# The small transfers of a recurrent attention chain, issued by GpSimd instead of ScalarE and SyncE

## The chip, the cores and the metric

The kernel runs on one core of a Trainium2 chip. The metric is the device time of one launch in microseconds. The core has five engines with instruction queues of their own: TensorE (PE; its weight loads are shown as PEld), VectorE (DVE), ScalarE (ACT), GpSimd (POOL) and SyncE (SP, which only issues transfers here). A transfer is issued by one of these queues and carried by 16 shared DMA engines. SPq, ACTq and POOLq in the profile are the issuing instructions of those queues.

## The reference

Two branches read the same normalised input `xn = layernorm(x)`, 2048 rows of 1024, and the result is `x + A(xn) + B(xn)`.

Branch A is attention with a recurrent memory over 64 segments of 32 rows:

```python
for s in range(64):
    h = concat([mem, xs])                     # 8 memory rows + 32 rows of the segment
    q, k, v = h@Wq, h@Wk, h@Wv                # 1024 -> 32 heads x 128
    p = softmax(mask(q@k.T * 128**-0.5))      # 40 x 40 per head
    o = (p@v) @ Wo
    mem = o[:8];  out[s] = o[8:]              # the memory of the next segment
```

Every segment needs the memory that the one before it produced, so the 64 segments are a chain. Each of the four weight matrices has 4096 x 1024 bf16 elements, 8.4 MB.

Branch B picks the 2 rows of `xn` with the highest score `xn@w_r`, passes them through a gated MLP (1024 to 3584 and back) and adds the two results to their rows.

## The kernel before

**Prologue.** Layer norm of 16 tiles of 128 rows, the transposes of `xn` and of `x + xn`, stored to DRAM as `xT_d` (segment inputs) and `zT_d` (the residual, to be added to each segment's output), then branch B, whose two rows are patched into `zT_d`.

**Weights.** The four matrices are cut into 64 granules of 128 x 2048 bf16 (512 KB). 42 stay in SBUF for the whole chain (tiles `wres`, `N_RES = 42`); the other 22 don't fit and are read from DRAM again in every segment, into tile `g`, a pool of six slots (`N_SLOT = 6`). Those 22 are spread evenly over the order of use. `used(g)` issues the next such load right after the matmuls of a streamed granule, so the queue of loads runs at most six ahead of their use. All these loads are issued by SP at line 248.

**One segment** (loop `for s in range(NSEG)`): six phases of eight granules, in the order Q first half, K first half, Q second half, K second half, V first half, V second half (`PHASES`); each granule is four matmuls (L510) that fill a `PSm` bank. Then the output projection with Wo, 16 granules (L549). Smaller steps hang between the granules as hooks, `hook(phase, kc, fn)`: they run after granule `kc` of that phase. The scores of the first 16 heads come at (2, 5), those of the second half at (4, 5); the weighted sums with V at (5, 2), (5, 5) and inside the Wo loop. At the end `OB` is copied from PSUM (L575, L576), its memory rows are transposed and put into the next segment's input `ST` (L267).

**Left rows.** A tile has 32 columns: 24 rows of the segment and 8 of the memory. The remaining 8 rows of four segments are put together as 32 "left" rows (`STL`) and projected for a whole group of four segments at a time. The position in a group is `j = s % 4`. In the segment with j = 1 the left rows of the next group go through Wq, with j = 2 through Wk (extra matmuls at L514), with j = 0 those of the own group go through Wv. The projected left rows are transposed (`transposes_left`, L421), copied to `QS` (L424, ACT), stored to DRAM in `qkl_d` (L426) and read back segment by segment as `QKL` (L357). `QKL` is read by a POOL copy into the right-hand columns of `KT` (L432), and the score matmuls (L436, L438) need that copy.

**The small transfers of the chain**, per segment: four stores of `OB` to the output (L579, 12 KB each), one load of the residual `ZT` (L394, 64 KB), one of the next input `ST` (L260, 64 KB), two of `QKL` (L357, 64 KB each). In two segments of four, two stores of `QS` (L426, 128 KB each); once per group a load of `STL` (L351, 64 KB) and four stores of `OL`, the left rows' output (L596, 16 KB each). Stores of outputs are issued by SP, between the weight loads; the others by ACT, between its PSUM copies.

**Order and waits.** The order on each engine is the order of the program text (`manual_schedule`), and every queue is strictly in order: an instruction that waits holds everything behind it. The completion of transfers is counted on semaphores. There are eight of them for the transfers that SP and ACT issue together (DMAHW0 to DMAHW7 in the order rows), and eight more for those of POOL (DMASW0 to DMASW7). They are handed out in turn, and a transfer waits before its issue until the one that had the same semaphore before it has landed.

Of the kernel before, what the change touches and what calls it, by code (L numbers as in the profile page):

```python
# [25 lines left out]
def kernel(  # L26
# [16 lines left out]
    nc = tc.nc  # L43
# [4 lines left out]
    SEG = int(A_seg_len)  # L48
# [8 lines left out]
    XM = SEG - M  # L57
# [4 lines left out]
    out2 = out[0]  # L62
# [32 lines left out]
    xT_d = [dram.tile([4, P, KC * SEG], BF16, name=f"xT_d{t}") for t in range(NT)]  # L95
    zT_d = dram.tile([NSEG + 1, P, KC, SEG], BF16, name="zT_d")
    stl_d = [dram.tile([P, KC * SEG], BF16, name=f"stl_d{t}") for t in range(NT)]
    qkl_d = [dram.tile([2, 2, P, 4, P], BF16, name=f"qkl_d{t}") for t in range(NT)]
# [158 lines left out]
        fetch()  # L257
    def load_st(s):
        ST = stp.tile([P, KC, SEG], BF16, tag="st", name="ST")
        nc.scalar.dma_start(out=ST.rearrange("p k r -> p (k r)"), in_=xT_d[s // 4][s % 4])  # L260
# [87 lines left out]

    def load_stl(g):
        STL = one.tile([P, KC, SEG], BF16, tag="stl", name="STL")  # L350
        nc.scalar.dma_start(out=STL.rearrange("p k r -> p (k r)"), in_=stl_d[g][:, :])  # L351
        return STL

    def load_qkl(s, half):

        t = two.tile([P, 2, P], BF16, tag="qkl", name="QKL")
        nc.scalar.dma_start(out=t[:, :, :], in_=qkl_d[s // 4][:, half, :, s % 4, :].rearrange("m p c -> p m c"))  # L357
# [12 lines left out]

    for s in range(NSEG):
# [19 lines left out]

        def fetch_z():
            Zt = nxt["z"] = one.tile([P, KC, SEG], BF16, tag="zt", name="ZT")
            nc.scalar.dma_start(out=Zt[:, :, :], in_=zT_d[s])  # L394

        def split_z():
            Zt = nxt["z"]
# [3 lines left out]
        def fetch_st():  # L401
            if s + 1 < NSEG:
                nxt["st"] = load_st(s + 1)
# [14 lines left out]
        def transposes_left(mat, half, XB, g):  # L418
            PTq = psT.tile([P, 4, 4, 32], BF16, tag="t", name="PTq")
            for il in range(4):  # L420
                nc.tensor.transpose(out=PTq[:, il, :, :].rearrange("p j r -> p (j r)"), in_=XB[:, il * P:(il + 1) * P],  # L421
                                    identity=IDENT[:, :])
            QS = two.tile([P, 4, 16, XL], BF16, tag="xb", name="QS")
            nc.scalar.copy(out=QS.rearrange("p s h r -> p h s r"),  # L424
                           in_=PTq.rearrange("p i j (s r) -> p (i j) s r", s=4))
            nc.scalar.dma_start(out=qkl_d[g][mat, half].rearrange("p s c -> p (s c)"),  # L426
                                in_=QS.rearrange("p s h r -> p (s h r)"))

        def scores(half):
            QKL = load_qkl(0, half) if s == 0 else QKLs.pop(0)  # L430
            q, k = QT[half], KT[half]
            nc.gpsimd.tensor_copy(out=k[:, :, 32:NK], in_=QKL[:, 1, :].rearrange("p (h r) -> p h r", r=XL))  # L432
# [70 lines left out]
        for p, (mat, half) in enumerate(PHASES):  # L503
            PSm = psA.tile([P, 512], F32, tag="acc", name="PSm")
            PSl = psL.tile([P, 512], F32, tag="accl", name="PSl") if mat in left else None
            for kc in range(KC):
                g = 8 * p + kc
# [12 lines left out]
            if mat < 2:  # L520
                XB = two.tile([P, 512], BF16, tag="xb", name="XB")
                nc.scalar.copy(out=XB[:, :], in_=PSm[:, :])  # L522
                hooks.setdefault((p + 1, 1), []).insert(0, lambda m=mat, h=half, b=XB: transposes(m, h, b))
                if PSl is not None:
                    XBl = two.tile([P, 512], BF16, tag="xb", name="XBl")
                    nc.vector.tensor_copy(out=XBl[:, :], in_=PSl[:, :])
                    hooks.setdefault((p + 1, 3), []).insert(
                        0, lambda m=mat, h=half, b=XBl, g=left[mat]: transposes_left(m, h, b, g))
            else:
                c0 = half * 512  # L530
                VM[half] = one.tile([P, 512], BF16, tag="vm", name="VM")
# [44 lines left out]
        nc.vector.tensor_copy(out=OB[:, P:256], in_=WO[:, P:256])  # L576
        def store(OB=OB, s=s):
            for g in range(4):
                nc.sync.dma_start(out=out2[s * SEG:s * SEG + XM, 256 * g:256 * (g + 1)],  # L579
                                  in_=OB[32 * g:32 * g + XM, :])  # L580

        todo = [store]
# [6 lines left out]
        if j == 3:  # L589
            OL = one.tile([P, 256], BF16, tag="pm", name="OL")  # L590
            nc.scalar.copy(out=OL[:, :], in_=WL[:, 0:256])

            def store_left(OL=OL, G=G):
                o4 = out2[4 * G * SEG:4 * (G + 1) * SEG, :].rearrange("(s r) d -> s r d", s=4)
                for g in range(4):
                    nc.sync.dma_start(out=o4[:, XM:SEG, 256 * g:256 * (g + 1)], in_=OL[32 * g:32 * (g + 1), :])  # L596
            todo.append(store_left)
        if s + 1 < NSEG:
            ST = nxt["st"]
# [37 lines left out]
```

## Time and profile before

| | |
|---|---|
| median of 3 runs | 2555.86 us (2551.04 to 2556.03) |
| the profiled execution | 2564.14 us, span 2562.2 us |
| PE busy | 1865.3 us, 73% of the span |
| ACT / DVE / POOL busy | 513.5 / 638.4 / 108.0 us |
| moved by DMA | 831.71 MB, mean 325 GB/s |
| of these, SP's queue (q1) and ACT's (q10) | 800.19 MB and 26.25 MB |
| first and last `OB` copy | 234.5 and 2553.9 us |

The profile's page has the totals, the queues, a chain of waits that leads to the end, and groups of instructions. Beside it the trace can be asked for waits by who waited for whom, for a timeline of one engine, and for the busy time and the transfer rate in chosen windows. In the windows the "DMA share" is the mean busy share of the 16 DMA engines; it can read a few hundredths over 1 because packets overlap. A busy PE is partly a matter of modelled ends, and a wait for several semaphores is put down to the one that came last.

### The profile page before, as it was taken

How to read it: one execution, taken by the hardware profiler on the slowest of the kernel's cores; microseconds unless marked ns; L12 is line 12 of the kernel's file. 1: busy time of each engine (PE TensorE's matmuls, PEld its weight loads, DVE VectorE, ACT ScalarE, POOL GpSimd, SP SyncE). 2: the span in 40 equal slices, each digit the busy share in tenths (PEclk: the TensorE clock that was granted, in tenths of full speed). 3: DMA queues.
4: the chain of work that ended last, by engine and by line, in shares of the span. 5: the costliest groups of instructions: out<-in, count | busy, mean ns of one | idle time of the engine just before them, and what ended most of it. 6: DMA issues, size and time to landing. Idle time of an engine off the chain costs nothing.

```text
span 2562.2 us, 82489 instructions
## 1 busy us (share of the span) xinstructions
PE 1865.3 (73%) x36873; PEld 975.1 (38%) x36873; DVE 638.4 (25%) x1733; ACT 513.5 (20%) x1145; POOL 108.0 (4%) x371
## 2 busy tenths in 40 slices
PE   4366777777777777677777777777776877777676
PEld 3233343344334334333433343343333433343333
DVE  5302222222222222222222222222232222222222
ACT  4202122121212212111221212122121221122111
POOL 4200000000000000000000000000000000000000
PEclk9568989898989989988898988999899988889889
DMA  9997999999999989989998999999998998999898
GB/s 333 298 353 244 341 320 323 316 351 340 311 332 326 340 297 328 335 299 334 329 349 302 344 322 321 341 330 339 313 334 309 360 320 302 334 327 340 320 336 293
DMA packets 368855, 831.71 MB, mean 325 GB/s; under 512 B 69458, under 2 KB 122738, under 8 KB 368500
## 3 DMA queue, kind: packets, MB, share of 16 engines
q1 hardware_dynamic: 303668, 800.19, 87.3%
q10 hardware_dynamic: 64832, 26.25, 3.8%
q8 instruction: 288, 4.72, 0.7%
q14 instruction: 67, 0.55, 0.1%
HBM read 804.28 MB, written 22.02 MB: 322 GB/s over the span
## 4 chain that ended last, share of the span: by engine, by line
DMA 62%; PE 27%; issue 4%; DVE 3%; ACT 2%; SPq 2%; ACTq 1%; POOL 0%; DVEq 0%; POOLq 0%
DMA g<-in_A_Wv_dram 15%; DMA g<-in_A_Wq_dram 14%; DMA g<-in_A_Wo_dram 13%; PE PSm L510 12%; DMA g<-in_A_Wk_dram 6%; PE WO L549 4%; PE PSl L514 3%; DMA qkl_d<-QS 2%; DMA QKL<-qkl_d 2%; PE WL L549 2%; DMA ZT<-zT_d 2%; PE PTq L408 1%; DMA ST<-xT_d 1%; SPq L248 1%; DMA zT_d<-Tz 1%
## 5 line engine op out<-in xcount | busy, mean ns | idle before, releaser
L510 PE MATMUL PSm<-wres,ST 128*32 128x512 bf16 x8192 | 785.2, 423 | 15.7 <-DVE ST L267 13.6
L510 PE MATMUL PSm<-g,ST 128*32 128x512 bf16 x4096 | 450.9, 427 | 325.8 <-DMA g<-in_A_Wk_dram 136.0
L510 PEld LDWEIGHTS <-ST 128*32 128x32 bf16 x12288 | 329.0, 101 | 770.2 <-issue 413.8
L549 PEld LDWEIGHTS <-OT 128*32 128x32 bf16 x8192 | 224.8, 102 | 170.5 <-issue 150.9
L522 ACT CAST XB<-PSm 128x512 bf16<-128x512 f32 x256 | 150.2, 587 | 660.6 <-PE PSm L510 535.2
L549 PE MATMUL WO<-wres,OT 128*32 128x256 bf16 x5120 | 248.2, 293 | 17.3 <-issue 17.3
L549 PE MATMUL WO<-g,OT 128*32 128x256 bf16 x3072 | 169.1, 294 | 99.6 <-DMA g<-in_A_Wo_dram 83.8
L514 PE MATMUL PSl<-wres,STL 128*32 128x512 bf16 x2048 | 210.4, 398 | 2.7 <-DMA STL<-stl_d 2.7
L488 ACT CAST OT<-OP 128x256 bf16<-128x256 f32 x256 | 95.5, 373 | 324.6 <-PE OP L485 324.6
L448 ACT ACTIVATE SPS<-SPS 128x320 f32<-128x320 f32 x128 | 54.0, 422 | 528.4 <-DVE SPS L447 503.7
L416 DVE COPY KT<-PTq 128x512 bf16<-128x512 bf16 x128 | 54.4, 425 | 348.9 <-PE PTq L408 348.6
L408 PE MATMUL PTq<-IDENT,XB 128*128 128x128 bf16 x1024 | 112.9, 240 | 35.6 <-ACT XB L522 33.6
L446 DVE TENSOR_REDUCE NM<-SPS 128x8 f32<-128x320 f32 x128 | 63.0, 492 | 302.0 <-PE SPS L441 302.0
L432 POOL COPY KT<-QKL 128x128 bf16<-128x128 bf16 x128 | 37.3, 291 | 2335.4 <-PE WO L549 1057.4
L490 DVE CAST OTL<-OP 128x64 bf16<-128x64 f32 x128 | 28.8, 225 | 406.8 <-ACT OT L488 406.8
L408 PEld LDWEIGHTS <-XB 128*128 128x128 bf16 x1024 | 64.2, 104 | 166.2 <-ACT XB L522 131.5
L413 DVE COPY QT<-PTq 128x512 bf16<-128x512 bf16 x128 | 53.2, 416 | 261.1 <-PE PTq L408 261.0
L514 PEld LDWEIGHTS <-STL 128*32 128x32 bf16 x3072 | 86.3, 100 | 70.8 <-issue 14.0
L483 PE MATMUL OP<-PT,VM 32*128 32x40 bf16 x2048 | 94.9, 180 | 19.3 <-ACT VM L532 14.4
L514 PE MATMUL PSl<-g,STL 128*32 128x512 bf16 x1024 | 105.2, 397 | 0.0
L483 PEld LDWEIGHTS <-VM 32*128 32x128 bf16 x2048 | 66.2, 92 | 94.9 <-issue 58.7
L485 PE MATMUL OP<-PT,VL 32*128 32x40 bf16 x2048 | 88.1, 176 | 4.2 <-ACT VL L534 4.2
(99 smaller groups left out, 1513.4 us busy)
## 6 DMA issues: line engine op xcount, KB each, us to landing
g<-in_A_Wq_dram SPq DMA_DIRECT2D x384, 512.0 KB
g<-in_A_Wo_dram SPq DMA_DIRECT2D x384, 512.0 KB
g<-in_A_Wk_dram SPq DMA_DIRECT2D x320, 512.0 KB
g<-in_A_Wv_dram SPq DMA_DIRECT2D x320, 512.0 KB
qkl_d<-QS ACTq DMA_DIRECT2D x64, 128.0 KB
QKL<-qkl_d ACTq DMA_DIRECT2D x128, 64.0 KB
g<-in_B_w_gate_dram SPq DMA_DIRECT2D x16, 448.0 KB
g<-in_B_w_up_dram SPq DMA_DIRECT2D x16, 448.0 KB
```

What stands on the lines that cost most here:

```text
L408: nc.tensor.transpose(out=PTq[:, il, :, :].rearrange("p j r -> p (j r)"), in_=XB[:, il * P:(il + 1) * P], identity=IDENT[:, :])
L413: nc.vector.tensor_copy(out=QT[half][:, :, :], in_=pv)
L416: nc.vector.tensor_copy(out=KT[half][:, :, 0:32], in_=pv)
L446: nc.vector.tensor_reduce(out=NM[:, :], in_=S8, axis=AX.X, op=ALU.max, negate=True)
L448: nc.scalar.activation(out=S8, in_=S8, func=ACTF.Exp, scale=SCALE)
L483: nc.tensor.matmul(o, lhsT=VM[half][q0:q0 + 32, il * P:(il + 1) * P], rhs=PTm[q0:q0 + 32, il, 0:NK], start=True, stop=False, tile_position ...
L485: nc.tensor.matmul(o, lhsT=VL[q0:q0 + 32, c0:c0 + P], rhs=PTl[q0:q0 + 32, il, 0:NK], start=False, stop=True, tile_position=(q0, 0), skip_g ...
L488: nc.scalar.copy(out=OT[half][:, 2 * ph:2 * ph + 2, :, :], in_=ov[:, :, :, 0:SEG])
L510: nc.tensor.matmul(PSm[32 * jq:32 * jq + 32, :], lhsT=ST[:, kc, :], rhs=Gv[:, 512 * jq:512 * (jq + 1)], start=(kc == 0), stop=(kc == KC - ...
L514: nc.tensor.matmul(PSl[32 * jq:32 * jq + 32, :], lhsT=STL[:, kc, :], rhs=Gv[:, 512 * jq:512 * (jq + 1)], start=(kc == 0), stop=(kc == KC - 1),
L522: nc.scalar.copy(out=XB[:, :], in_=PSm[:, :])
L549: nc.tensor.matmul(PS[32 * g:32 * g + 32, 0:256], lhsT=lhs(h), rhs=Gv[:, D * hs + 256 * g:D * hs + 256 * (g + 1)], start=False, stop=(last ...
```

## The change

Seven `dma_start` calls move to the GpSimd queue, with the same operands and at the same places of the program:

```diff
 def load_st(s):
-    nc.scalar.dma_start(out=ST..., in_=xT_d[s // 4][s % 4])
+    nc.gpsimd.dma_start(out=ST..., in_=xT_d[s // 4][s % 4])
 def load_stl(g):
-    nc.scalar.dma_start(out=STL..., in_=stl_d[g][:, :])
+    nc.gpsimd.dma_start(out=STL..., in_=stl_d[g][:, :])
 def load_qkl(s, half):
-    nc.scalar.dma_start(out=t[:, :, :], in_=qkl_d[s // 4][:, half, :, s % 4, :]...)
+    nc.gpsimd.dma_start(out=t[:, :, :], in_=qkl_d[s // 4][:, half, :, s % 4, :]...)
 def fetch_z():
-    nc.scalar.dma_start(out=Zt[:, :, :], in_=zT_d[s])
+    nc.gpsimd.dma_start(out=Zt[:, :, :], in_=zT_d[s])
 def transposes_left(mat, half, XB, g):
-    nc.scalar.dma_start(out=qkl_d[g][mat, half]..., in_=QS...)
+    nc.gpsimd.dma_start(out=qkl_d[g][mat, half]..., in_=QS...)
 def store(OB=OB, s=s):            # four per segment
-    nc.sync.dma_start(out=out2[...], in_=OB[32 * g:32 * g + XM, :])
+    nc.gpsimd.dma_start(out=out2[...], in_=OB[32 * g:32 * g + XM, :])
 def store_left(OL=OL, G=G):       # four per group
-    nc.sync.dma_start(out=o4[...], in_=OL[32 * g:32 * (g + 1), :])
+    nc.gpsimd.dma_start(out=o4[...], in_=OL[32 * g:32 * (g + 1), :])
```

PE's and DVE's instructions stay in the order they had. What follows are the order rows of SP and POOL at two places, with the waits that each instruction carries.

SP around the start of the second segment (s = 1), before. `g` is a streamed granule, `OB` the output of the segment that has just ended; PE in the brackets is the release of the slot.

```order
L248 DMA g<-in_A_Wq_dram 128x2048 [waits DMAHW2_49,PE_49]
L248 DMA g<-in_A_Wq_dram 128x2048 [waits DMAHW3_49,PE_49]
L579 DMA out_dram<-OB 24x256 [waits DVE_49]
L579 DMA out_dram<-OB 24x256 [waits DMAHW4_49]
L579 DMA out_dram<-OB 24x256 [waits DMAHW5_49]
L579 DMA out_dram<-OB 24x256 [waits DMAHW6_49]
L248 DMA g<-in_A_Wq_dram 128x2048 [waits DMAHW7_49,PE_49]
L248 DMA g<-in_A_Wk_dram 128x2048 [waits DMAHW1_49,PE_49]
L248 DMA g<-in_A_Wk_dram 128x2048 [waits DMAHW4_49,PE_49]
L248 DMA g<-in_A_Wk_dram 128x2048 [waits DMAHW5_49,DMAHW0_49,PE_49]
```

The same place of the changed kernel:

```order
L248 DMA g<-in_A_Wq_dram 128x2048 [waits DMAHW6_49,PE_49]
L248 DMA g<-in_A_Wq_dram 128x2048 [waits DMAHW7_49,PE_49]
L248 DMA g<-in_A_Wq_dram 128x2048 [waits DMAHW0_49,PE_49]
L248 DMA g<-in_A_Wk_dram 128x2048 [waits DMAHW1_49,PE_49]
L248 DMA g<-in_A_Wk_dram 128x2048 [waits DMAHW2_49,PE_49]
L248 DMA g<-in_A_Wk_dram 128x2048 [waits DMAHW3_49,PE_49]
```

SP has nothing but weight loads left there, and since only they use the eight DMAHW semaphores now, each one waits for the load eight places before it; before, the numbers skip where an ACT transfer had taken a semaphore in between.

POOL in the third segment of a group (s = 2, j = 2), before. `KT<-QKL` is the copy that the score matmuls need, first half and second half.

```order
L432 COPY KT<-QKL 128x16x8 [waits DVE_49,DMAHW7_49,PE_49,Activation_49]
L456 MEMSET PL 128x8x8 [waits DVE_49]
L432 COPY KT<-QKL 128x16x8 [waits DVE_49,DMAHW7_49,PE_49,Pool_49]
L398 COPY ZL<-ZT 128x8x8 [waits DMAHW1_49]
L399 MEMSET ZT 128x8x8 [waits Pool_49]
```

The same segment in the changed kernel; four stores of `OB` (L579) stand directly ahead of the first row.

```order
L394 DMA ZT<-zT_d 128x256 [waits DMASW3_49,PE_49,Pool_49]
L426 DMA qkl_d_120<-QS 128x512 [waits DMASW4_49,Activation_49]
L260 DMA ST<-xT_d_86 128x256 [waits DMASW5_49]
L432 COPY KT<-QKL 128x16x8 [waits PE_49]
L456 MEMSET PL 128x8x8
L357 DMA QKL<-qkl_d_119 128x2x128 [waits DMASW6_49,PE_49,Pool_49]
L426 DMA qkl_d_120<-QS 128x512 [waits DMASW7_49,Activation_49]
L432 COPY KT<-QKL 128x16x8 [waits DVE_49]
L357 DMA QKL<-qkl_d_119 128x2x128 [waits DMASW0_49,PE_49,Pool_49]
L398 COPY ZL<-ZT 128x8x8 [waits DMASW3_49]
L399 MEMSET ZT 128x8x8 [waits Pool_49]
```

Both `KT` copies now stand behind a store of `QS` that waits for an ACT copy of the same phase. (In the after rows the copy's wait for a transfer is not always listed, because POOL has already waited for it earlier in its own order.)

More of the change, by code (lines that the diff above doesn't have):

```diff
@@ L259, in load_st @@
         ST = stp.tile([P, KC, SEG], BF16, tag="st", name="ST")
-        nc.scalar.dma_start(out=ST.rearrange("p k r -> p (k r)"), in_=xT_d[s // 4][s % 4])
+        nc.gpsimd.dma_start(out=ST.rearrange("p k r -> p (k r)"), in_=xT_d[s // 4][s % 4])
         return ST
@@ L350, in load_stl @@
         STL = one.tile([P, KC, SEG], BF16, tag="stl", name="STL")
-        nc.scalar.dma_start(out=STL.rearrange("p k r -> p (k r)"), in_=stl_d[g][:, :])
+        nc.gpsimd.dma_start(out=STL.rearrange("p k r -> p (k r)"), in_=stl_d[g][:, :])
         return STL
@@ L356, in load_qkl @@
         t = two.tile([P, 2, P], BF16, tag="qkl", name="QKL")
-        nc.scalar.dma_start(out=t[:, :, :], in_=qkl_d[s // 4][:, half, :, s % 4, :].rearrange("m p c -> p m c"))
+        nc.gpsimd.dma_start(out=t[:, :, :], in_=qkl_d[s // 4][:, half, :, s % 4, :].rearrange("m p c -> p m c"))
         return t
@@ L425, in transposes_left @@
                            in_=PTq.rearrange("p i j (s r) -> p (i j) s r", s=4))
-            nc.scalar.dma_start(out=qkl_d[g][mat, half].rearrange("p s c -> p (s c)"),
+            nc.gpsimd.dma_start(out=qkl_d[g][mat, half].rearrange("p s c -> p (s c)"),
                                 in_=QS.rearrange("p s h r -> p (s h r)"))
@@ L578, in store @@
             for g in range(4):
-                nc.sync.dma_start(out=out2[s * SEG:s * SEG + XM, 256 * g:256 * (g + 1)],
+                nc.gpsimd.dma_start(out=out2[s * SEG:s * SEG + XM, 256 * g:256 * (g + 1)],
                                   in_=OB[32 * g:32 * g + XM, :])
@@ L595, in store_left @@
                 for g in range(4):
-                    nc.sync.dma_start(out=o4[:, XM:SEG, 256 * g:256 * (g + 1)], in_=OL[32 * g:32 * (g + 1), :])
+                    nc.gpsimd.dma_start(out=o4[:, XM:SEG, 256 * g:256 * (g + 1)], in_=OL[32 * g:32 * (g + 1), :])
             todo.append(store_left)
```

## The prediction

> **What bounds the kernel now.** I read the page first, then SP's waits, the chain, and windows over a few segments.
>
> ```profile
> span 2562.2 us, 82489 instructions
> L510 PE MATMUL PSm<-g,ST 128*32 128x512 bf16 x4096 | 450.9, 427 | 325.8 <-DMA g<-in_A_Wk_dram 136.0
> L549 PE MATMUL WO<-g,OT 128*32 128x256 bf16 x3072 | 169.1, 294 | 99.6 <-DMA g<-in_A_Wo_dram 83.8
> q1 hardware_dynamic: 303668, 800.19, 87.3%
> q10 hardware_dynamic: 64832, 26.25, 3.8%
> L575 ACT CAST OB<-WO x64: 266/267/268, 234.5 to 2553.9; 128x128 bf16<-128x128 f32 x64
> ```
>
> The last row gives the pace: 63 segments in 2553.9 - 234.5 = 2319.4 us, **36.8 us a segment**. PE idles 325.8 + 99.6 = 425 us ahead of matmuls that use streamed weights, 6.6 us a segment; it is late weights, not arithmetic, that PE waits for. Without that a segment's PE path is 36.8 - 6.6 = 30.2 us. The question is why the weights are late, when their queue runs six granules ahead. The windows are one gap-free stretch, one hole at a segment's start, and four whole segments (j = 0, 1, 2, 3); the last three columns are PE clock, DMA share and GB/s.
>
> ```profile
> 1296.00:1312.00 16.00, 11.98 (x286) 6.90 (x289) 2.94 (x11) 3.71 (x10) 0.38 (x2) 1.00 1.04 397
> 1278.00:1281.00 3.00, 2.61 (x44) 1.01 (x36) 0.34 (x1) 1.17 (x2) 0.00 (x0) 1.00 0.63 194
> 1235.00:1272.00 37.00, 29.05 (x610) 15.30 (x609) 8.44 (x24) 7.44 (x17) 0.77 (x5) 0.86 0.90 315
> 1272.00:1307.00 35.00, 27.19 (x556) 13.75 (x548) 9.74 (x26) 7.53 (x17) 1.00 (x5) 0.95 1.00 357
> 1307.00:1343.00 36.00, 28.18 (x555) 14.15 (x548) 9.74 (x26) 7.53 (x17) 1.00 (x5) 0.91 0.95 334
> 1343.00:1381.00 38.00, 27.36 (x607) 14.76 (x597) 8.96 (x26) 6.62 (x16) 1.39 (x7) 0.91 0.95 342
> ```
>
> The engines can move 397 GB/s, but not through a segment, because there are holes. The hole at 1278 is made as follows (SP's timeline, then the chain at the same place):
>
> ```profile
> 1271.98 2.81 SPq L248 DMA_DIRECT2D g<-in_A_Wq_dram  x2
> 1274.84 3.33 SPq L579 DMA_DIRECT2D out_dram<-OB  x4
> 1279.15 0.37 SPq L248 DMA_DIRECT2D g<-in_A_Wq_dram  x1
> ```
>
> ```profile
> 1271.32 6.53 DMA g<-in_A_Wk_dram
> 1277.86 1.98 DMA out_dram<-OB
> ```
>
> SP issued two loads by 1274.8, then the four output stores. The last store was issued at 1277.86, at the end of the first chain row: a weight load had to land first, since the store waits for a semaphore. The next weight load followed at 1279.15. For over 4 us no weights were ordered. The second chain row leads on to an issue of ACT, which waited for an output store in the same way. The totals of SP's waits (total, times, longest):
>
> ```profile
> SPq L248 <- PE PSm L510: 311.7, 364, 6.2
> SPq L248 <- DMA qkl_d<-QS: 174.6, 48, 8.8
> SPq L248 <- DMA QKL<-qkl_d: 136.7, 60, 5.1
> SPq L248 <- DMA ZT<-zT_d: 57.2, 26, 3.5
> SPq L248 <- DMA out_dram<-OB: 26.0, 26, 2.6
> SPq L579 <- DMA g<-in_A_Wk_dram: 66.3, 61, 3.5
> ```
>
> The first row is the wait that has to be: PE has not released the slot. The next four, 174.6 + 136.7 + 57.2 + 26.0 = 394 us, have nothing to do with the weights. A load stands still until a small transfer of ACT or an output store has landed, because both had the same one of eight semaphores. The last row is the store's own wait, with loads behind it.
>
> **What the change removes.** SP keeps only weight loads; each then waits for its slot and for the load eight places back, which has landed whenever a six-slot ring has room. So the 394 us, and the stores' 66, go from SP's queue. They are not gains one for one, since SP is often ahead; what they buy is a stream without holes. The price of a segment is then the larger of two floors.
>
> *Transfers.* The four windows moved 37 x 315 + 35 x 357 + 36 x 334 + 38 x 342 = 49,170 KB, 12.29 MB a segment. At 397 GB/s, the upper bound, that is 31.0 us; at 357, the best whole segment, 34.4. That segment has all kinds of small transfers in it and one hole, 3 us at a share of 0.63, so 1.1 us lost. Without it 35 x 357 / 33.9 = 369 GB/s. I take 369, since it is the same mix: **33.3 us**.
>
> *PE.* 30.2 us, plus what the change adds (below). So the transfers bound, and the gain is 36.8 - 33.3 = 3.5 us, over 63 segments **-220 us**.
>
> The rule of the Trainium skill that speaks against this is in DMA: Bandwidth & Descriptors, section Issuing engines are not separate DMA queues: transfers run on the same 16 engines whoever issues them, so another issuer saves only the sequencer's time. By that rule the sum would be the rival "nothing to gain" below; SP's rows of waits show that the issuer's place in a queue holds up more than its own time here.
>
> **What it adds.** Ten or so POOL issues a segment, of a kind the trace doesn't have. Bounds from the nearest rows: below, the same transfers on SP; above, POOL's longest instruction.
>
> ```profile
> L579 SPq DMA_DIRECT2D out_dram<-OB x256: 302/352/1460, 237.1 to 2556.8; - x128
> L596 SPq DMA_DIRECT2D out_dram<-OL x64: 615/618/773, 352.2 to 2559.3; - x64
> L168 POOL TENSOR_TENSOR XP<-XP,XN 128x1024 bf16<-128x1024 bf16 x16 | 33.9, 2118 | 42.2 <-ACT XN L163 42.2
> ```
>
> Between 0.35 and 2.1 us; I take **x = 1.0 us**, nearer to the issue rows because it is the same work of writing out addresses. For the software path the Trainium skill, DMA: Bandwidth & Descriptors, section Latency and other measured facts, gives about 1 us to the first byte against 0.6; no run here shows it yet.
>
> POOL's time of ten such issues is hidden: it is busy 1.0 us of a 35 us segment (x5 in the windows). What counts is what stands behind them in its queue, the `KT` copies:
>
> ```profile
> 1307.38 0.29 POOL L432 COPY KT<-QKL 128x128 bf16<-128x128 bf16 x1 [22.98 <-DMA g<-in_A_Wq_dram]
> 1316.44 0.59 ACT L424 COPY QS<-PTq 128x512 bf16<-128x512 bf16 x1 [1.51 <-PE PTq L421]
> 1317.37 0.20 PE L436 MATMUL SPS<-KT,QT 128*32 128x40 bf16 x4
> 1326.60 0.59 ACT L424 COPY QS<-PTq 128x512 bf16<-128x512 bf16 x1 [1.68 <-PE PTq L421]
> 1326.88 0.19 PE L436 MATMUL SPS<-KT,QT 128*32 128x40 bf16 x4
> ```
>
> Before, the first copy ran at 1307.4, right when the segment began, 10 us ahead of the scores (1317.4). In an ordinary segment it now follows four stores, `ZT` and `ST`: 6x + 0.3 = 6.3 us, still in time. In the third segment of a group (this one, j = 2) it follows the store of `QS`, which can't be issued before `QS` is copied (1317.03), and the `ST` load: ready at 1317.03 + 2x + 0.3 = 1319.3, so the scores are **2.0 us late**. The second copy, behind the next `QS` store, is ready at 1327.19 + x + 0.3 = 1328.5, **1.6 us late**. 3.6 us in each of 15 such segments: 54 us of PE time, whose path there becomes 30.2 + 3.6 = 33.8 against the transfers' 33.3. Loads go on while PE stands, until six slots are full, so about half of it shows: **+25 us** (bounds 0 and 54). The reads of `QKL`, `ZT`, `ST` and `STL` are ordered several us or a segment ahead, and a start 1 us later is hidden by the phases between.
>
> The ends are exposed. At s = 0 the first `QKL` is stored and read back while the scores wait, two transfers each about 1.5 us slower: +3. At the end:
>
> ```profile
> 2554.54 2.67 SPq L579 DMA_DIRECT2D out_dram<-OB  x4
> 2557.31 2.63 SPq L596 DMA_DIRECT2D out_dram<-OL  x4
> ```
>
> Eight issues in 5.4 us become eight in 8: +3. ACT loses its issues, which took it little, and its waits for semaphores with them; I credit nothing, as it bounds nothing.
>
> **The sum**, against the profiled execution's own 2564: 2564 - 220 + 25 + 6 = 2375. That execution is 2564.14 - 2555.86 = 8 us above the median of the runs, so **2367 us**, 7% faster.
>
> **The rivals.**
>
> *The stream was at its limit already* (faster, but little). q1 and q10 together fill 91.1% of the engines' time, and two of the four windows read 334 and 342 GB/s at a share of 0.95. If closing the holes only makes more transfers compete, the rate stays near 342 and a segment costs 35.9 us: 0.9 x 63 = 57 us less, 2564 - 57 + 31 - 8 = 2530. For it: the 16 us at 397 had hardly a small transfer in them. Against: the window at 1272 has them all and reaches 357.
>
> *GpSimd becomes the bound* (slower). The place is the first `KT` copy. It is late in ordinary segments from 6x + 0.3 > 10, x = 1.6, and PE's path reaches the old 36.8 us when the delay is 6.6: x = 2.7 is where it decides. At x = 3 it is 18.3 - 10 = 8.3 us late, 30.2 + 8.3 = 38.5 a segment, +1.7 x 63 = 107, with 20 for the ends 2564 + 127 - 8 = 2683. For it: POOL is one queue, and nothing in it may pass an issue. Against: x would lie above the upper row. The mechanism that could bring it there is VectorE, busy 9.74 of 35 us in the window at 1272, if its copies keep POOL from writing descriptors. In the Trainium skill, SBUF — State Buffer, section Who interferes with whom, a VectorE copy in a two-port mode shuts GpSimd out, and a software transfer of about 620 ns is said to have taken 3100 ns beside one. No trace here shows such a pair yet.
>
> *Nothing to gain* (the change does what it says, but SP's waits were harmless). SP saves 256 x 0.352 + 64 x 0.618 = 130 us of its own time, and a segment keeps 36.8 us because PE's releases, the 311.7 row, take the place of the semaphores: 2564 + 31 - 8 = 2587 with what is added, 2556 if that is hidden. Against: the hole at 1278 ends with a load that stood behind stores, and at the releases alone SP waited less than at the semaphores (311.7 against 394).
>
> That it doesn't do what it says is excluded: the order rows show the stores and loads in POOL's queue and none in SP's.
>
> **Chances.** Forecast (2290 to 2450) 0.63; stream at its limit (2450 to 2550) 0.17; GpSimd the bound 0.12; nothing to gain 0.08, split evenly between the same and slower. About 0.2% is what a measurement of this kernel can tell from no change: 2551 to 2561. So faster 0.80, same 0.04, slower 0.16. The range: 31.0 us a segment for the transfers and PE's 30.2 can't both be met without either waiting for the other now and then; half-way between 31.0 and 33.3, 32.2 a segment, gives 2564 - 290 + 31 - 8 = 2297, and I put the low end at 2290. The high end, 2550, takes in the second case.
>
> **What would show it.** In the profile of the changed kernel: a queue of software descriptors with q10's packets and the stores', q10 left with the four loads of the initial memory; POOL's issues with their durations, which decide x; SP's waits with only PE rows at L248 and none for `qkl_d`, `QKL`, `ZT` or `out`; no hole at the segment's start; a pace of 33 to 34 us; PE's idle time ahead of L510 and L549 on `g` cut to less than half of 425 us. Wrong steps would show as follows: the rate, by segments without holes at 340 GB/s and PE still waiting for `g`; x, by POOL issues over 1.6 us and a large row of PE at L436 waiting for POOL's L432; the third segments, by that row with about 15 x 3.6 us if right. The prediction as a whole is wrong if SP's waits for small transfers vanish and the pace doesn't move.

## The result and the profile after

The changed kernel takes 2307.23 us (median of 4 runs, 2291.36 to 2311.28) against 2555.95 us of the kernel before beside it: a ratio of **0.9016 [0.8969, 0.9063]**, 249 us less. The forecast was 2367 us with a range of 2290 to 2550.

From the page after: the span, the queues, the two groups of matmuls on streamed weights and the groups of the new POOL issues.

```profile
span 2309.0 us, 82539 instructions
q1 hardware_dynamic: 292148, 795.98, 93.2%
q0 software_dynamic: 22016, 30.48, 3.9%
q10 hardware_dynamic: 64, 0.02, 0.0%
...
L510 PE MATMUL PSm<-g,ST 128*32 128x512 bf16 x4096 | 421.1, 398 | 111.7 <-DMA g<-in_A_Wq_dram 52.8
L549 PE MATMUL WO<-g,OT 128*32 128x256 bf16 x3072 | 164.6, 285 | 66.4 <-DMA g<-in_A_Wo_dram 53.8
L579 POOL DMA_DIRECT2D out_dram<-OB x256 | 130.4, 516 | 662.9 <-DVE OB L576 662.8
L357 POOL DMA_DIRECT2D QKL<-qkl_d x128 | 91.8, 717 | 520.3 <-issue 377.9
L426 POOL DMA_DIRECT2D qkl_d<-QS x64 | 36.2, 565 | 449.8 <-ACT QS L424 437.4
```

All small transfers went to the software queue; ACT's queue kept the load of the initial memory alone. PE's idle time ahead of streamed weights fell from 425 to 111.7 + 66.4 = 178 us. An issue on POOL takes 0.52 to 0.72 us.

The pace, from the first and last copy of `OB` after:

```profile
L575 ACT CAST OB<-WO x64: 266/266/268, 229.5 to 2297.0; 128x128 bf16<-128x128 f32 x64
```

63 segments in 2067.5 us, **32.8 us each** (before 36.8, 2319.4 us). The profiled executions took 2564.14 and 2310.86 us, 253 us apart, and 252 of them lie between these two copies. Outside them the stretch up to the first copy is 5.0 us shorter and the one behind the last copy 3.7 us longer (12.0 against 8.3 us).

The same long window of the loop, before and after (busy time of PE, PEld, DVE, ACT, POOL, then PE clock, DMA share, GB/s):

```profile
235.00:2220.00 1985.00, 1497.91 (x30124) 769.92 (x30124) 490.50 (x1350) 391.39 (x899) 54.25 (x268) 0.90 0.93 327
```

```profile
235.00:2220.00 1985.00, 1560.45 (x33854) 828.18 (x33847) 545.90 (x1511) 428.97 (x1010) 419.90 (x920) 0.96 1.00 368
```

The rate rose from 327 to 368 GB/s; a segment moves the same, 36.8 x 327 = 12.03 MB before and 32.8 x 368 = 12.07 MB after. The granted clock rose from 0.90 to 0.96. SP's waits after:

```profile
SPq L248 <- PE PSm L510: 539.7, 656, 7.1
SPq L248 <- PE PSl L514: 261.0, 190, 10.3
SPq L248 <- PE WO L549: 198.6, 258, 4.0
...
SPq L248 <- DMA g<-in_A_Wk_dram: 87.5, 141, 2.8
```

No row is left for `qkl_d`, `QKL`, `ZT` or `out_dram` at L248. In their place SP waits longer for PE (311.7 and 166.3 us before at the first and third row). Here this is good news: SP stands with the next load in hand and the ring full. Its own loads are still among its waits: the four rows of Wq, Wo, Wk and Wv make 93.1 + 89.0 + 87.5 + 68.8 = 338 us (355 before). In the trace after, all 594 of these waits end with the landing of the load six places back, the one that fills the same slot. So the load that the order rows after make a load wait for is the sixth before it, not the eighth, as the text beside those rows and the prediction have it; nothing in the sum hangs on that.

The hole at a segment's start is gone too. The windows around two starts after read 332 and 317 GB/s, where the hole before read 194; the poorest of the windows of 3 us at those two starts reads 281, at a DMA share of 0.92 against 0.63:

```profile
1218.00:1222.00 4.00, 2.98 (x48) 1.25 (x45) 0.48 (x2) 0.85 (x2) 2.96 (x6) 1.00 0.93 332
1250.00:1256.00 6.00, 5.26 (x130) 3.24 (x122) 0.66 (x3) 1.07 (x3) 4.37 (x8) 1.00 0.96 317
```

The cost that the change adds stands in the waits of PE after. Most of it is the `KT` copy behind the store of `QS`; below it POOL's timeline in a third segment:

```profile
PE SPS L436 <- POOL KT L432: 60.4, 33, 7.2
```

```profile
1194.05 0.56 POOL L426 DMA_DIRECT2D qkl_d<-QS  x1 [7.95 <-ACT QS L424]
1194.59 0.54 POOL L260 DMA_DIRECT2D ST<-xT_d  x1
1195.12 0.30 POOL L432 COPY KT<-QKL 128x128 bf16<-128x128 bf16 x1
```

### The profile page after: what moved, and what is told of

It is laid out like the page before. It is cut to its first block, busy times and chain, and to the rows that moved or that the text cites. A ratio compares the mean times of both kernels' runs of the same rounds, so it can differ in the third digit from the quotient of the medians.

```text
span 2309.0 us, 82539 instructions
## 1 busy us (share of the span) xinstructions
PE 1739.3 (75%) x36873; PEld 937.0 (41%) x36873; DVE 635.7 (28%) x1733; ACT 502.6 (22%) x1145; POOL 488.9 (21%) x1027
## 3 DMA queue, kind: packets, MB, share of 16 engines
q0 software_dynamic: 22016, 30.48, 3.9%
## 5 line engine op out<-in xcount | busy, mean ns | idle before, releaser
L510 PE MATMUL PSm<-wres,ST 128*32 128x512 bf16 x8192 | 733.2, 397 | 16.4 <-DVE ST L267 13.6
L510 PE MATMUL PSm<-g,ST 128*32 128x512 bf16 x4096 | 421.1, 398 | 111.7 <-DMA g<-in_A_Wq_dram 52.8
L510 PEld LDWEIGHTS <-ST 128*32 128x32 bf16 x12288 | 309.0, 98 | 480.7 <-issue 195.1
L549 PEld LDWEIGHTS <-OT 128*32 128x32 bf16 x8192 | 218.2, 100 | 138.3 <-issue 123.2
L579 POOL DMA_DIRECT2D out_dram<-OB x256 | 130.4, 516 | 662.9 <-DVE OB L576 662.8
L549 PE MATMUL WO<-wres,OT 128*32 128x256 bf16 x5120 | 243.4, 286 | 28.8 <-issue 28.7
L549 PE MATMUL WO<-g,OT 128*32 128x256 bf16 x3072 | 164.6, 285 | 66.4 <-DMA g<-in_A_Wo_dram 53.8
L357 POOL DMA_DIRECT2D QKL<-qkl_d x128 | 91.8, 717 | 520.3 <-issue 377.9
L408 PE MATMUL PTq<-IDENT,XB 128*128 128x128 bf16 x1024 | 104.5, 226 | 63.2 <-ACT XB L522 59.9
L408 PEld LDWEIGHTS <-XB 128*128 128x128 bf16 x1024 | 59.5, 99 | 187.7 <-ACT XB L522 173.6
L426 POOL DMA_DIRECT2D qkl_d<-QS x64 | 36.2, 565 | 449.8 <-ACT QS L424 437.4
```

Of the source, the lines that this page charges most:

```text
L357: nc.gpsimd.dma_start(out=t[:, :, :], in_=qkl_d[s // 4][:, half, :, s % 4, :].rearrange("m p c -> p m c"))
L510: nc.tensor.matmul(PSm[32 * jq:32 * jq + 32, :], lhsT=ST[:, kc, :], rhs=Gv[:, 512 * jq:512 * (jq + 1)], start=(kc == 0), stop=(kc == KC - ...
L549: nc.tensor.matmul(PS[32 * g:32 * g + 32, 0:256], lhsT=lhs(h), rhs=Gv[:, D * hs + 256 * g:D * hs + 256 * (g + 1)], start=False, stop=(last ...
L579: nc.gpsimd.dma_start(out=out2[s * SEG:s * SEG + XM, 256 * g:256 * (g + 1)], in_=OB[32 * g:32 * g + XM, :])
```

## The experiments

### Which of the moves gives the gain

`e1_stores_pool` is the kernel before with the eight stores alone on GpSimd (`out_dram<-OB`, L579, and `out_dram<-OL`, L596); `e2_loads_pool` is the changed kernel with those stores back on SP.

```diff
 # e1, from the kernel before          # e2, from the changed kernel
-nc.sync.dma_start(out=out2[...       -nc.gpsimd.dma_start(out=out2[...
+nc.gpsimd.dma_start(out=out2[...     +nc.sync.dma_start(out=out2[...
 (and the same at out=o4[...)           (and the same at out=o4[...)
```

> Only the output stores (L579, L596) go to GpSimd; ACT keeps the loads and the QS store. Theory (weight loads are held by small transfers, by standing behind stores and by the eight semaphores shared with ACT): SP loses the stores' own waits (66 + 18 + 11 us) and the 26 us for out, but keeps those for qkl_d, QKL, ZT and ST (378 us), so most of the gain is missing: about 2450 us, 0.96 of before. Rival A (only the place of the stores ahead of the loads mattered): as fast as the whole change, about 2310. Rival B (only the shared semaphores mattered): 2530 to 2560, hardly faster than before.

> The complement: ACT's transfers (ST, STL, ZT, QKL, QS) go to GpSimd, the output stores stay on SP between the weight loads. Theory: the 378 us of SP's waits for ACT's transfers go, the stores' place and their waits for a weight load's semaphore stay; about 2400 us, 0.94 of before, with the hole at the start of a segment still there. Rival A (only the stores' place mattered): 2530 to 2560. Rival B (only the semaphores shared with ACT mattered): as fast as the whole change, about 2310.

Measured: stores alone 2371.98 us, 0.9239 [0.9167, 0.9312], some 80 us faster than I had expected and between that and the first rival; the ACT transfers alone 2399.67 us, 0.9342 [0.9263, 0.9421], as expected. The kernel before took 2562.03 us beside them, so they gain 190 and 162 us. Together they give 249, not 352: the two edits free the same queue, and what one has freed the other can't free again. (Beside the experiments the kernel before had medians of 2559 to 2566 us, on three chips; a difference of two kernels from different chips is good to some 10 us.)

The waits of SP in e1 show what stayed:

```profile
SPq L248 <- DMA qkl_d<-QS: 131.2, 50, 6.7
SPq L248 <- DMA QKL<-qkl_d: 121.7, 69, 4.8
SPq L248 <- DMA ZT<-zT_d: 114.9, 40, 5.9
SPq L248 <- DMA ST<-xT_d: 98.2, 32, 6.1
```

These are 466 us, more than the 394 us of before, and yet e1 is only 65 us slower than the changed kernel. So the sum of these waits does not price them.

In e2 the stores hardly wait themselves; first its SP timeline at the start of a group, then SP's and PE's waits, then the two groups of the changed kernel for comparison:

```profile
1164.71 1.61 SPq L579 DMA_DIRECT2D out_dram<-OB  x4
1166.41 0.36 SPq L248 DMA_DIRECT2D g<-in_A_Wq_dram  x1
1166.87 3.29 SPq L596 DMA_DIRECT2D out_dram<-OL  x4
1170.26 1.34 SPq L248 DMA_DIRECT2D g<-in_A_Wk_dram  x3
```

```profile
SPq L248 <- DMA g<-in_A_Wk_dram: 154.3, 196, 2.1
...
PE PSm L510 <- DMA g<-in_A_Wk_dram: 72.2, 63, 4.8
PEld L510 <- DMA g<-in_A_Wk_dram: 69.3, 37, 5.3
```

```profile
L510 PE MATMUL PSm<-g,ST 128*32 128x512 bf16 x4096 | 421.1, 398 | 111.7 <-DMA g<-in_A_Wq_dram 52.8 <-DMA g<-in_A_Wv_dram 32.2 <-DMA g<-in_A_Wk_dram 22.5
L510 PEld LDWEIGHTS <-ST 128*32 128x32 bf16 x12288 | 309.0, 98 | 480.7 <-issue 195.1 <-DMA g<-in_A_Wk_dram 24.3 <-DVE ST L267 20.6
```

PE waits 72.2 + 69.3 = 141.5 us for Wk weights in e2 and 22.5 + 24.3 = 46.8 in the changed kernel: 95 us more, and e2 is 92 us slower (83 by the ratios). That the two come so close is partly chance, since other waits rose as well (Wv from 32.2 to 50.5 us, "issue" ahead of the weight loads of PE from 195.1 to 256.2). The loads behind the stores are late. Part of it is plain issue time (1.61 and 3.29 us for four stores); part is that each store takes a turn of the eight semaphores, so that a weight load behind four stores waits for a load only four places back. In the trace of e2 157 of SP's waits, 128 us, end with the load four places back, and none in the changed kernel; SP's own Wk row rose from 87.5 to 154.3 us. How the 92 us split between the two parts was not tried.

### The issuer, with the same transfers

`e3_stores_act` puts the stores on ScalarE: out of SP's queue, but still on the shared semaphores.

```diff
-nc.sync.dma_start(out=out2[...      (and out=o4[...)
+nc.scalar.dma_start(out=out2[...
```

> The output stores move from SP to ACT's queue instead, with hardware descriptors; SP then has weight loads alone, as in the changed kernel, but all small transfers still share its eight semaphores. Theory (shared semaphores count, whoever issues): SP's waits for small transfers stay near 400 us, and ACT's copies now stand behind the stores' waits too; no faster than the stores on GpSimd, 2480 to 2580. Rival A (only the place in SP's queue mattered): about the same as with the stores on GpSimd, and both near 2310.

Measured: 2441.95 us, 0.951 [0.9435, 0.9586]; faster than the theory's 2480 to 2580, and far from the rival's 2310. SP's waits, and the new one of ACT:

```profile
SPq L248 <- DMA QKL<-qkl_d: 152.6, 51, 5.9
SPq L248 <- DMA out_dram<-OB: 133.2, 75, 5.8
SPq L248 <- DMA qkl_d<-QS: 126.8, 47, 5.7
```

```profile
ACT XB L522 <- DMA out_dram<-OB: 108.7, 24, 5.8
```

The weight loads now wait for the stores by semaphore (133.2 us, 26.0 before), and ACT's copies stand behind its own issues. Even so, 2562.03 - 2441.95 = 120 us are gained: that is the worth of the place in SP's queue, less what ACT's new waits cost. On GpSimd the same stores gain another 70 us (2371.98). There they have semaphores of their own, a queue with little else in it and software descriptors; what each of these is worth was not separated.

By the Trainium skill, DMA: Bandwidth & Descriptors, section Issuing engines are not separate DMA queues, the choice of issuer saves the sequencer's time alone. The measurement differs: with the stores issued by SP, ACT and POOL the kernel takes 2562.03, 2441.95 and 2371.98 us, and SP's whole time of issuing them, 130 us by the prediction's rows, is less than the 190.

### What the shared semaphores alone cost

`e11_tiny_act` takes the changed kernel and issues on ACT a load of 512 bytes at each place of a former ACT transfer, but for the one of `STL`. Nothing reads these loads. They only take turns of the semaphores between the weight loads.

```diff
+    PAD = const.tile([P, 16], BF16, name="PAD")
+    def tiny():
+        nc.scalar.dma_start(out=PAD[r:r + 16, :], in_=A_mem0[0, 0:1, 0:256]...)
 def load_st(s):                     # and load_qkl, fetch_z, transposes_left
+    tiny()
     nc.gpsimd.dma_start(...)
```

> The changed kernel with one very small extra load (512 bytes) on ACT's queue at the place of each former ACT transfer but STL's, five or so a segment. It moves nothing to speak of, but takes a turn of the eight semaphores that the weight loads use. Theory (sharing the semaphores with another queue is a cause by itself): most of the 65 us by which the kernel with only the stores on GpSimd is behind comes back, 2345 to 2375, and SP's waits show PAD rows. Rival (it was the bigger ACT transfers themselves, their size or time to land): within 15 us of 2307.

Measured: 2329.48 us, 0.9094 [0.9046, 0.9142], between the two expectations. SP's waits show the turns at work:

```profile
SPq L256 <- DMA PAD<-in_A_mem_dram: 300.5, 142, 6.0
```

300 us of SP's waits cost 22 us of time by the medians; by the ratios, 0.9094 - 0.9016, it is 20 us, give or take 17. e1 is 65 us behind the changed kernel (57 by the ratios, give or take 22), so the turns explain about a third of that, and hardly all. The rest belongs to what a tiny load doesn't have of a real ACT transfer (its time to land, and how long ACT stands behind its issue); which of these it is was not separated.

### The stall that the change adds

`e5_kt_first` is the changed kernel with each `KT` copy moved ahead of the `QS` store of its phase, three granules before the scores. Everything else stays.

```diff
+        def kt_left(half):
+            QKL = QKT[half] = load_qkl(0, half) if s == 0 else QKLs.pop(0)
+            nc.gpsimd.tensor_copy(out=KT[half][:, :, 32:NK], in_=QKL[:, 1, :]...)
         def scores(half):
-            QKL = load_qkl(0, half) if s == 0 else QKLs.pop(0)
+            if s == 0: kt_left(half)
+            QKL = QKT.pop(half)
             q, k = QT[half], KT[half]
-            nc.gpsimd.tensor_copy(out=k[:, :, 32:NK], in_=QKL[:, 1, :]...)
...
+        if s > 0:
+            hook(2, 2, lambda: kt_left(0))
+            hook(4, 2, lambda: kt_left(1))
```

> The changed kernel with the KT copies moved ahead of the QS store in GpSimd's queue (hooks at granule 2 instead of 5 of the phase). Theory (transfers bind, so PE's 60 us of waiting for late KT copies are hidden behind them): the row of PE at L436 waiting for POOL's L432 falls from 60 us to about 10, the pace stays at 32.8 us, time within 0.5% of the changed kernel's 2307. Rival (those waits show, as the prediction's +25 us had them): 25 to 50 us faster, 2257 to 2282.

Measured: **2269.27 us, 0.8853 [0.882, 0.8885]**, 38 us faster than the changed kernel and the fastest kernel of this study with the whole computation. My theory fell, the rival was right. The row of the wait, the pace and the loop's window in e5:

```profile
PE SPS L443 <- POOL KT L433: 14.6, 3, 7.4
```

```profile
L585 ACT CAST OB<-WO x64: 266/266/267, 230.7 to 2242.1; 128x128 bf16<-128x128 f32 x64
```

```profile
235.00:2230.00 1995.00, 1589.26 (x34873) 849.24 (x34869) 562.84 (x1561) 441.46 (x1040) 430.88 (x946) 0.97 1.01 379
```

The pace is (2242.1 - 230.7) / 63 = 31.9 us. Between the profiled executions the loop is 2067.5 - 2011.4 = 56 us shorter, by the medians the whole is 38 us shorter, and the wait is 60.4 - 14.6 = 46 us less: the stall shows about one for one, within some 10 us either way. And the rate went from 368 to 379 GB/s, so the DMA share of 1.00 in the changed kernel was no proof that the transfers were at their limit.

### The floor of PE

`e4_half_weights` (from the changed kernel) and `e8_half_kt_first` (from e5) load only half of each streamed granule and use that half twice; half of the streamed weights is left out of the computation, the matmuls are as many as before.

```diff
-nc.sync.dma_start(out=granule_out(t, what[1]), in_=granule_dram(what[1]))
+nc.sync.dma_start(out=t[:, 0:1024], in_=granule_dram(what[1])[:, 0:1024])   # Wo: its first half likewise
...
-rhs=Gv[:, 512 * jq:512 * (jq + 1)]
+rhs=Gv[:, 512 * (jq % 2):512 * (jq % 2 + 1)]                                # streamed granules only
```

> The changed kernel with only the first half of each streamed weight granule of the chain loaded (256 KB instead of 512 KB); the matmuls are the same in number and shape and read that half twice, so part of the weights is left out of the computation. Theory (the changed kernel is at the transfer rate, 0.99 busy at 364 GB/s): the pace falls from 32.8 us a segment to PE's path, 30 us or a little less, so 2110 to 2180 us. Rival (PE's own chain of waits sets the 32.8 us): within 30 us of 2310.

> Half of each streamed granule loaded, as in the run with half weights (half of the weights is left out of the computation), and the KT copies first. There transfers don't bind (share 0.61), so the late copies must show: 1987 minus up to 60, 1925 to 1960. If it stays at 1985, PE's waits for KT are no loss even where PE binds.

Measured: 1987.53 us, 0.7752 [0.7676, 0.7828], and 1940.63 us, 0.7573 [0.7528, 0.7619]. The loop of e4, its pace and its wait for `KT`:

```profile
235.00:1970.00 1735.00, 1482.89 (x34986) 824.50 (x34982) 564.27 (x1566) 442.12 (x1046) 428.25 (x941) 0.99 0.73 227
```

```profile
L579 ACT CAST OB<-WO x64: 265/265/266, 225.0 to 1972.3; 128x128 bf16<-128x128 f32 x64
```

```profile
PE SPS L439 <- POOL KT L435: 62.1, 33, 6.3
```

With the transfers at a share of 0.73 a segment takes 27.7 us, and 27.0 with the copies first (the same row of e8 runs from 230.4 to 1929.9). That is PE's path at a clock of 0.99. The prediction had 30.2, and e4's expectation 30 or a little less, so e4 came out more than 120 us faster than the range given for it. (The share of 0.61 in e8's expectation came from a window that ran on past the end of e4.) With half of the weights the early copies are worth 47 us and with all of them 38: the stall costs about the same whether the transfers bound or PE does.

### When GpSimd becomes the bound

`e6_pad12` and `e7_pad24` put 12 and 24 small memsets on GpSimd ahead of each transfer that it issues, to raise x, the time that an issue holds POOL.

```diff
+    def pad():
+        for _ in range(12):                    # 24 in e7
+            nc.gpsimd.memset(PAD[:, :], 0.0)   # 128 x 16, bf16
 def store(OB=OB, s=s):                         # and the other six calls
     for g in range(4):
+        pad()
         nc.gpsimd.dma_start(...)
```

> The changed kernel with 12 very small memsets ahead of each GpSimd transfer of the chain, about 0.1 us each, so that an issue takes about 1.7 us of the queue instead of 0.55. Theory (PE's path is 27.8 us and has 5 us to spare under the transfers' 32.8): KT is ready 6 x 1.7 + 0.3 = 10.5 us after the segment's end instead of 3.6, about 3 to 4 us late, still hidden: 2300 to 2360. Rival (GpSimd's queue is on the path already): every us shows, 2500 or more.

> The same with 24 memsets, so about 2.9 us an issue. Theory: KT is ready 17.7 us after the segment's end, some 10 us late, PE's path is about 38 us and binds: 2600 to 2700, slower than before, the prediction's second rival come true above its point of 2.7 us. If it stays below 2400, the price of a slow issue was put too high.

Measured: 2825.19 us, 1.1026 [1.0957, 1.1095], and 3665.98 us, 1.4307 [1.4223, 1.4391]. Both are far above what I expected, and the rival named for e6 was right: little of the delay is hidden. The memsets took more than I had reckoned; the distance between issues gives x, in e6 1007.17 - 1004.54 = 2.63 us, in e7 1011.62 - 1006.99 = 4.63:

```profile
1004.54 0.53 POOL L591 DMA_DIRECT2D out_dram<-OB  x1 [9.65 <-DVE OB L587]
1007.17 0.53 POOL L591 DMA_DIRECT2D out_dram<-OB  x1
```

```profile
1006.99 0.51 POOL L591 DMA_DIRECT2D out_dram<-OB  x1
...
1011.62 0.51 POOL L591 DMA_DIRECT2D out_dram<-OB  x1
```

PE's wait for the copy, e6 and then e7:

```profile
PE SPS L447 <- POOL KT L443: 510.5, 64, 16.7
```

```profile
PE SPS L447 <- POOL KT L443: 1307.4, 64, 35.1
```

So 8.0 us a segment in e6 and 20.4 in e7, 12.4 / 2.0 = 6.2 us for each microsecond of x. This is a mean over segments that differ. In e6's trace six issues stand ahead of the first copy at j = 3, seven at j = 1 and j = 2 (one store of `QS` more) and ten at j = 0 (the four stores of `OL`), and the mean wait is 4.1, 5.7, 7.4 and 15.2 us at j = 3, 1, 2 and 0. PE's timeline in e6 for one segment with j = 0 and for the one with j = 3 in the same group:

```profile
1029.79 0.23 PE L447 MATMUL SPS<-KT,QT 128*32 128x40 bf16 x4 [13.98 <-POOL KT L443]
...
1147.31 0.21 PE L447 MATMUL SPS<-KT,QT 128*32 128x40 bf16 x4 [2.57 <-POOL KT L443]
```

The pace, from the same rows of the `OB` copy as above, is 40.8 and 53.7 us, 6.4 per microsecond of x. Followed back in a straight line, which is an estimate, the old pace of 36.8 is reached at x = 2.0 and the changed kernel's 32.8 at x = 1.4. GpSimd's issues of 0.52 to 0.72 us lie under both.

### The ring on the far side

The ring of slots and the resident weights share SBUF: one slot more is one granule less that stays. Both kernels start from e5.

```diff
-N_RES = 42                 # 43 in e9, 41 in e10
-N_SLOT = 6                 #  5 in e9,  7 in e10
```

> KT copies first, and one granule more resident with one slot less (43 and 5): 21 streamed granules a segment instead of 22, 4.5% less traffic, one load less in flight. If the amount moved sets the 31.9 us a segment of the KT-first kernel, the pace falls by up to 1.4 us: 2180 to 2220 us. If the six loads in flight do (a ring that runs dry whenever PE stands), it gets slower: 2290 to 2350.

> The other way: 41 resident and 7 slots, 23 streamed granules, 4.5% more traffic with one load more in flight. Amount moved sets the pace: up to 1.4 us more a segment, 2330 to 2360. Depth of the ring sets it: faster than the KT-first kernel's 2269.

Measured: 2312.59 us, 0.9037 [0.8986, 0.9088], and 2319.22 us, 0.9046 [0.8994, 0.9098]; both slower than e5. e9 lies where the depth of the ring was to put it, e10 a little under the range for the amount moved. Their windows, e9 and then e10:

```profile
235.00:2230.00 1995.00, 1580.22 (x34346) 839.10 (x34342) 551.75 (x1528) 434.42 (x1024) 427.13 (x935) 0.97 0.98 356
```

```profile
235.00:2230.00 1995.00, 1571.47 (x33789) 828.54 (x33785) 544.47 (x1509) 426.85 (x1007) 418.54 (x916) 0.96 1.01 381
```

With 21 streamed granules in place of 22, e9 has some 0.5 MB a segment less to move, and gets only 356 GB/s: five slots are too few. e10 has 0.5 MB more, and its seven slots reach 381, hardly more than e5's 379: there the rate no longer grows with depth and the bytes decide. Six slots lie between the two.

## Why the prediction was right, and where its numbers were off

**The cause was right.** The weight loads were held up by what stood between them, not by the DMA engines. Most signs that the prediction named came: the software queue with the bytes of ACT's queue and of the stores (though in 22,016 packets, where ACT's queue alone had 64,832), no row of SP left for a small transfer, no hole at a segment's start, and PE's idle time ahead of streamed weights at 178 us, less than half of 425. Two came otherwise. SP's waits are not for PE alone, 338 us are for its own loads; and the pace, 32.8 us, lies below the 33 to 34 named.

**The sum was 64 us short.** It has -220 + 25 + 6 = -189 us; the profiled executions differ by -253. By its terms (e5's profiled execution was 13 us under its median, so the first two lines are good to about that):

| term | predicted | measured | from |
|---|---|---|---|
| the stream without holes | -220 | -308 | loop before, 2319.4, less that of e5, 2011.4 |
| late `KT` copies in third segments | +25 | +56 | loop after, 2067.5, less that of e5 |
| the ends | +6 | -1 | 2564.14 - 2319.4 = 244.7 before, 2310.86 - 2067.5 = 243.4 after |

That the first two errors have opposite signs is luck: the late copies cost 31 us more than forecast and hid a third of what the stream gained beyond the forecast.

*The stream* was mis-sized by 88 us, in two factors. The bytes: the four windows with 12.29 MB a segment end at 1381, but the trace has the fourth segment's copy of `OB` at 1378.8, so they took in 2 us of a fifth. From copy to copy, 1234.7 to 1378.8, the rate is 335 GB/s, which is 12.07 MB a segment, and the long window gives 12.05 (12.03 before, 12.07 after). At the predicted 369 GB/s that is 32.7 us, not 33.3, and 0.65 x 63 = 41 us. The rate: 369 was read in the best segment with its hole taken out, and the changed kernel shows 368, but with the third segments' stalls in it. Without them e5 gets 379, which is the other 47 us.

*The late copies*: the mechanism and its place were right. In the trace 30 of the 33 waits are the two of each of 15 third segments, 45.7 us together, where 54 was predicted; of the rest 13.8 us are at s = 0, where PE waited 10.7 us before the change too. That the size is so near is partly luck. With an issue of 0.55 us in place of 1.0 the prediction's working gives 1.1 + 1.2 us a segment, some 33 us. The remainder is in two things that it left out: POOL's store starts 0.3 us after the copy of `QS` ends (1193.75 and 1194.05), and in the first of the two PE now asks for the scores before that copy has ended (1193.61), where before it asked 0.3 us behind it. Wrong was the step "loads go on while PE stands, so about half of it shows". About all of it shows: 38 us by the medians and 56 by the profiled executions, for 46 us of waits (e5; e8 likewise). Why the loads don't make up for it was not tried by itself; that a standing PE frees no slot would do it.

*The ends*: the +6 was added from two costs, and both came, at least in part. At the start PE's wait for the first `KT` copies at s = 0 grew from 10.7 to 13.8 us, near the +3 for two transfers of 1.5 us more each, a figure that no row stood behind. The end grew by 3.7 us, but not by its issues: eight of them took POOL 4.4 us, SP 5.4 (a store of `OL` takes 0.605 against 0.618 us; the row is in the last section). What grew is the time from the start of the last issue to the end of the span, 2309.0 - 2301.7 = 7.3 us after and 2562.2 - 2559.3 = 2.9 before. The net is -1 because the prologue was shorter: the first scores begin at 196.3 us after and at 203.1 before. In e1 to e5 they begin anywhere from 193.2 to 200.5, so a good part of that is scatter.

**PE's path** was put at 30.2 us by taking the idle time ahead of streamed weights off the pace. e4 and e8 measure 27.7 and 27.0. What the subtraction left in was matmuls at a lower granted clock (0.90 in the loop before, 0.99 in e4) and waits for weights that stand in other rows, such as 122.6 us of PEld at L510 for Wk (24.3 after). It did no harm, because 33.3 was above 30.2 and 31.9 is above 27.0: the larger of the two floors was the same.

**The rivals.** *The stream at its limit* (2530) is out: the same kinds of transfers moved at 368, then 379 GB/s, where it had 342. *GpSimd the bound* did not come, since x was 0.52 to 0.72 us, but e6 and e7 show its mechanism, at the place that it was given. Its point of decision was put too high, 2.7 against 2.0. Its deadline of 10 us was right for the ordinary segment that it priced (j = 3): in e6's trace PE asks for the scores 10.8 us after the segment's start there, the copy is ready at 14.8, and the mean wait is 4.1. What it left out are the seven and ten issues ahead of the copy in the other three segments of a group. And it let the delay first fill the gap between 30.2 and 36.8, while in e6 the wait came on top of the changed kernel's 32.8: 8.0 us of wait, 40.8 us of pace. Its price at x = 3, 38.5 us a segment, would have been about 40.8 + 0.37 x 6.4 = 43. VectorE did not stretch the issues, as the next section shows. *Nothing to gain* is out: PE's releases did take the place of the semaphores in SP's waits, as it said (539.7 us against 311.7), while the time fell by 249 us.

**The 394 us of waits** were named as what goes, not as the gain, and this was well: e1 keeps 466 us of them and is 65 us behind, e11 has 300 and is 22 behind. What the experiments add is an order. Moving the stores is worth more than moving ACT's transfers (190 against 162 us alone, 92 against 65 on top of the other), and turns of the semaphores taken by tiny loads cost least, some 20 us. How much of the rest is the place in a queue, the time that a transfer takes to land, or ACT standing, was not separated.

## What to carry to other kernels

A long stream of loads wants a queue and semaphores to itself: look in the waits of the issuing queue for rows that name some other transfer, and in short windows for holes in the rate, and price the cure by the bytes of a long window, or of windows that end where segments end, over the rate that the stream has outside the holes, not by the sum of those waits. Small transfers moved to another engine's queue bring their order with them: list what then stands behind them, and count a late copy there in full. If the deadline can be met by moving that copy a few steps ahead, do it in the same edit (here 38 us more, 2269.27 us).

## What the runs showed of the hardware

**GpSimd's issues are short and steady.** The durations of its stores after, least, median and most:

```profile
L579 POOL DMA_DIRECT2D out_dram<-OB x256: 505/513/547, 230.4 to 2299.3; - x128
L596 POOL DMA_DIRECT2D out_dram<-OL x64: 587/605/653, 335.3 to 2301.7; - x64
```

The Trainium skill, SBUF — State Buffer, section A bandwidth-pool intuition that's wrong (but worth ruling out), has a software transfer take about 3100 ns beside a copy on VectorE, in place of about 620. None of these 320 shows it, although VectorE is busy 28% of the span and copies `OB`, from PSUM, just ahead. Whether any of its copies here is of a kind that holds GpSimd up was not tried, so this does not speak against the page.

**A DMA share of 1.00 is no limit of the rate.** The loop reads 1.00 at 368 GB/s after, 1.01 at 379 in e5 and 1.01 at 381 in e10.

**The granted clock goes with the gaps in PE's work, on average.** In mean over the span it is 0.782 in e7, 0.836 in e6, 0.883 before, 0.932 after, 0.949 in e5 and 0.963 in e4, in the order of their times; e8, the fastest, has 0.956 and falls out of that order, and so does e11 with 0.945. From before to after the 128x512 matmul on streamed weights went from 427 to 398 ns, and PE's busy time as a whole from 1865.3 to 1739.3 us with the same 36,873 matmuls: about half of the difference between the two profiled executions, which no term of the prediction had. In the mean this agrees with the Trainium skill, TensorE: Matmul & The Clock Gate, Part 1, by which the gate is set by how busy PE has been of late. How much of the 249 us is clock and how much waiting can't be told apart here, since the one comes with the other.
